# Second halves of an h block behind an eviction, a queue of weight sums that yields, norm parts in scratch columns: one change to a fused attention, mixture and SwiGLU kernel

## The chip, the cores and the metric

One core of one Trainium2 chip runs the whole program in one launch. The metric is device time in microseconds (us), the median over runs; lower is better. Five engines run their own instruction streams and wait for each other on semaphores: TensorE (PE, its weight loads PEld), VectorE (DVE), ScalarE (ACT), GpSimd (POOL) and SyncE (SP, which here only issues DMAs).

## The reference

Causal attention with a local or a strided mask on 4x8 heads of 576 tokens, then a dense mixture of 8 experts whose gate is balanced by Sinkhorn steps (layer 1), then RMS norm and SwiGLU (layer 2). The 2304 tokens of 512 features run through

```
h = np.maximum(x @ w1[e], 0.0)              # layer 1: 8 experts, 512 -> 1024 -> 512
out += P[:, e:e+1] * (h @ w2[e])
rms = np.sqrt(np.mean(x * x, axis=-1) + 1e-6)
xn = x / rms * rms_g                        # norm
g, val = xn @ w_gate, xn @ w_val            # layer 2: 512 -> 1536 -> 512
return (g / (1 + np.exp(-g)) * val) @ w_out
```

Products are taken to float32's precision: each operand is a high and a low part, and three matmuls (high x high, high x low, low x high) make one product.

## The kernel before, in words

Attention and expert 0 come first; experts 1 to 7 and layer 2 then run in one loop over *quads*. A quad (g, qd) is expert or pass g on a third qd of the tokens (768, six tiles of 128, laid out as 2x2 blocks of 384 columns and 256 features). Layer 1 has 7 x 3 quads; layer 2 has 3 passes (g = 8, 9, 10) x 3 quads. A Strassen-like scheme computes four h blocks of 128 x 384 with seven products instead of eight: that is a *chain*, and the table `PROD` says for each of its seven products, here called product 0 to 6, which sum of weight blocks (`w1t`, `w1x`: "w1 sums") and which sum of x blocks (`xt`, `xx`: seven slots, loaded from the scratch tensor `xnd` in device memory in layer 2) it takes, and into which of two PSUM banks (`ub`) it adds. Consecutive chains swap the banks, and the next chain starts to write a bank as soon as the last reader of the old chain is through with it.

`outcome` runs behind each product. Products 0, 2 and 3 only have their bank copied away by ScalarE (`keep`). Behind products 1, 4, 5 and 6 an h block is finished: its number n is 0, 2, 1 and 3. In layer 1 that is an *add* of bank and keep on VectorE (n = 0, 2, 1; block 3 is read from the bank itself), a *high* part with relu on ScalarE, and a *low* part, the difference, on VectorE. In layer 2 a *round* is two chains. The g chain makes an add, a sigmoid on ScalarE and a product with it on VectorE; the v chain makes an add, a product with the g chain's block ("mul", L1084), a high part on ScalarE and a low part on VectorE (L1033). The engine that is asked for the second half of a block stands right behind the first in program order, whatever else it could do meanwhile.

The twelve products of a round's h blocks with w2 ("downs", L701 to L703, banks `db` 0 to 5) are laid between the products of the next round. So a quad's last downs run in the first round of the next quad, and VectorE *evicts* the six banks (L1465, L1476) into `acc` there. Everything else is pumped from queues, one slot after every product and down: `prep` makes the next chain's w1 sums from raw weights that GpSimd's DMAs bring (seven VectorE steps a block), `prep2` makes w2 parts, `conv` converts float64 weights, and `norm` does the norm steps between the layers: for each tile m of a quad, sums `ta`, `tb` and their high and low parts (VectorE, ScalarE, GpSimd), stored to `xnd` by SP. Behind expert 7 these parts lie in two free x slots before the store; the x loads of the next quad go into the same slots, so they wait until the stores have read them.

The lines of the profile that the next parts use: product L1019; add L1062 (layer 1), L1071 (g) and L1082 (v); mul L1074 (g) and L1084 (v); low part L1037 (layer 1) and L1033 (v); keep copies L1047; w1 sums L860 and L863; x loads L950; norm parts L1129, norm stores L1137 and L1156.

Of the kernel before, what the change touches and what calls it, by code (L numbers as in the profile page):

```python
# [22 lines left out]


class Background:


    def __init__(self):
        self.tasks = []
        self.queues = []  # L30
        self.now = 0

# [34 lines left out]
class Queue:  # L67


    def __init__(self, clock):  # L70
        self.clock = clock
        self.items = []
        self.last = 0
        clock.queues.append(self)
# [4 lines left out]
    def run(self):  # L79
        self.last = min(max(self.last + self.items[0][1], self.clock.now - 1), self.clock.now)  # L80
        self.items.pop(0)[2]()

    def pump(self):
        while self.items and self.last + self.items[0][1] < self.clock.now:
            self.run()

    def drain(self, tag):
        while any(x[0] == tag for x in self.items):
            self.run()


@with_exitstack
def kernel(
# [22 lines left out]
    NG = 4  # L116
# [71 lines left out]
    prep, prep2, conv = Queue(bg), Queue(bg), Queue(bg)  # L188
# [516 lines left out]
    def up(ps, w, x, n):  # L705
        for c in range(KC):
# [6 lines left out]
            )  # L713
            if c % 2:
                bg.pump()

    def down(accs, h, w, first, last, t):
# [6 lines left out]
        )  # L724

# [62 lines left out]
    def convert(nm, f, half):  # L788
# [15 lines left out]
        def head():  # L804
# [3 lines left out]
            )  # L808

        def number():  # L810
# [6 lines left out]
            )  # L817

        def tail():
# [3 lines left out]
            )  # L823

        def whole():
            nc.vector.tensor_tensor(out=t, in0=a.bitcast(F32), in1=t, op=ALU.add)

# [18 lines left out]
    def combine(s, raw):  # L846
# [18 lines left out]
        def first():  # L865
            round_(raw[:, :512], 0, 2)
            sum_(s1, a21, a22, ALU.add)

        def second():
            round_(a22, 2, 1)  # L870
            rest(a11, 0, 1)
            rest(a12, 1, 1)

        def third():
            sum_(a21, a11, a21, ALU.subtract)
            sum_(s2, s1, a11, ALU.subtract)

        def fourth():
            round_(tmp, 3, 2)
            rest(a22, 2, 1)  # L880
            sum_(a12, a12, s2, ALU.subtract)

        def fifth():
            round_(a21, 5, 1)
            rest(tmp, 3, 2)

        def sixth():
            round_(a12, 6, 1)
            rest(a21, 5, 1)

        def seventh():
            rest(a12, 6, 1)

# [29 lines left out]
    def prepare_2(g, f):  # L923
# [12 lines left out]
        def low():  # L936
            nc.vector.tensor_tensor(out=w2t[:, i, 1], in0=t, in1=w2t[:, i, 0].bitcast(F32), op=ALU.subtract)

# [77 lines left out]
    def product(ps, w, x, first):  # L1016
        for c in range(2):
            for n, (i, k) in enumerate(((0, 0), (0, 1), (1, 0))):
# [3 lines left out]
                )  # L1022

# [4 lines left out]
    def scratch(i):  # L1028
        return fa[:, 3200 + TH * i : 3200 + TH * (i + 1)] if i < 5 else cv[:, TH * (i - 5) : TH * (i - 4)]

    def put(src, h):
        nc.scalar.activation(h[0], src, AF.Copy)
        nc.vector.tensor_tensor(out=h[1], in0=src, in1=h[0].bitcast(F32), op=ALU.subtract)  # L1033

    def put_relu(src, h):
        nc.scalar.activation(h[0], src, AF.Relu)  # L1036
        nc.vector.scalar_tensor_tensor(  # L1037
            out=h[1], in0=src, scalar=0.0, in1=h[0].bitcast(F32), op0=ALU.max, op1=ALU.subtract
        )

    def outcome(i, a, b, use):


        keep = [fa[:, 2048 + TH * n : 2048 + TH * (n + 1)] for n in range(3)]
        a, b = a[:, :TH], b[:, :TH]
        if i in (0, 2, 3):
            nc.scalar.copy(keep[(0, None, 1, 2)[i]], b if i == 3 else a)  # L1047
        elif i == 1:
            use(0, b, keep[0])
        elif i == 4:  # L1050
            use(2, a, keep[2])
        elif i == 5:
            use(1, b, keep[1])
# [3 lines left out]
    def hidden_1(hs):  # L1057
# [9 lines left out]
    def hidden_g():  # L1067
# [10 lines left out]
    def hidden_v(hs):  # L1078
        def use(n, ps, more):
            src, to = ps, scratch(5 + n % 2)  # L1080
            if more is not None:
                nc.vector.tensor_tensor(out=to, in0=ps, in1=more, op=ALU.add)  # L1082
# [7 lines left out]
    def norm_scale(t0):  # L1090
# [6 lines left out]
        def mean():  # L1097
            nc.vector.tensor_scalar(out=ss, in0=ss, scalar1=1.0 / DM, scalar2=1e-6, op0=ALU.mult, op1=ALU.add)

# [3 lines left out]
        def xn(t):  # L1103
            nc.vector.tensor_scalar(
                out=acc[:, t0 + t], in0=acc[:, t0 + t], scalar1=ss[:, t : t + 1], scalar2=None, op0=ALU.mult
            )

# [3 lines left out]
    def norm_turn(ps, t):  # L1111
# [5 lines left out]
        )  # L1117

    def norm_blocks(qd, i, spare, close):
# [3 lines left out]
        ta, tb = cv[:, 768:1024], cv[:, 1024:1280]  # L1123
        sa, sb, sc = *spare, xt_flat[:, 7680:8192]
# [6 lines left out]
        def plain():  # L1131
            parts(xa, sa[:, :512], sa[:, 768:1280])
            parts(b22, sa[:, 512:768], sa[:, 1280:1536])

# [521 lines left out]
```

## Time and profile before

| what | us |
|---|---|
| median of 3 runs (2116.95 to 2119.74) | 2118.75 |
| span of the profiled execution | 2113.9 |
| TensorE busy | 2076.4 (98%) |
| VectorE busy | 1215.6 (58%) |
| ScalarE busy | 747.2 (35%) |
| GpSimd busy | 333.0 (16%) |

The profiled execution has no time of its own beside its span; the median of the runs is 4.85 us above it, and that difference stands for what lies around the span. "Busy" is an engine's time in instructions. TensorE's matmuls are pipelined: one of 128 x 384 is drawn 0.33 us long, but the next starts 0.174 us after it, so a busy TensorE is not one at its peak, and an idle gap that the trace draws is shorter than the delay behind it.

### The profile page before, as it was taken

To read this page: it belongs to the slowest core of one execution; us is meant where nothing else is said; L and a number is where in the kernel's file an instruction comes from. 1 tells how busy PE (TensorE), PEld (TensorE's weight loads), DVE (VectorE), ACT (ScalarE), POOL (GpSimd) and SP (SyncE) were. 2 spreads that over 40 slices of the span, in tenths; PEclk is the share of its full clock that TensorE was granted. 3 is DMA by queue.
4 is the path that set the end of the run, shared out by engine and by line. 5 is a ranking of instruction groups with operands and counts; after the bars stand their busy time and mean duration, and the time that the engine had idled before them with its cause. 6 is when DMAs were issued, how large, how long until landed. Compare 5 with 4: busy or idle time off the path is not lost.

```text
span 2113.9 us, 30671 instructions
## 1 busy us (share of the span) xinstructions
PE 2076.4 (98%) x11343; PEld 1853.1 (88%) x11343; DVE 1215.6 (58%) x2669; ACT 747.2 (35%) x1763; POOL 333.0 (16%) x503
## 2 busy tenths in 40 slices
PE   8999999999999999999999999999999999999999
PEld 7888888888888888888888988888988799888888
DVE  4777647557446644754664466455357665546645
ACT  7856323223223322322332233223244444423322
POOL 6444211123101200210120021001012100100000
PEclk9999999999999999999999999999999999999999
DMA  7685565553355253434623552552265674254242
GB/s 195 171 217 144 163 217 168 192 175 107 120 169 167 73 184 130 148 120 136 199 85 131 166 167 77 172 192 60 85 180 160 228 239 145 71 188 146 99 165 90
DMA packets 293861, 319.24 MB, mean 151 GB/s; under 512 B 80016, under 2 KB 215376, under 8 KB 293712
## 3 DMA queue, kind: packets, MB, share of 16 engines
q1 hardware_dynamic: 271568, 247.86, 37.5%
q0 software_dynamic: 22144, 69.42, 10.5%
q8 instruction: 89, 1.46, 0.3%
q14 instruction: 60, 0.49, 0.1%
HBM read 237.78 MB, written 79.43 MB: 150 GB/s over the span
## 4 chain that ended last, share of the span: by engine, by line
PE 83%; DVE 9%; ACT 3%; DMA 2%; issue 2%; SPq 0%; POOL 0%; DVEq 0%; ACTq 0%; POOLq 0%
PE ub L1019 36%; PE db L702 12%; PE db L703 12%; PE db L701 12%; PE psh L701 2%; PE psh L702 1%; PE psh L703 1%; DVE cv L1084 1%; PE psy L701 1%; PE ps_s L471 1%; PE psy L702 1%; PE psy L703 1%; DVE acc L1465 1%; DVE cv L1082 1%; PE ps_o L540 1%
## 5 line engine op out<-in xcount | busy, mean ns | idle before, releaser
L1019 PE MATMUL ub<-xt,w1t 128*128 128x384 f32 x2000 | 494.9, 339 | 15.5 <-DVE cv L1084 4.7
L1019 PEld LDWEIGHTS ub<-xt,w1t 128*128 128x128 f32 x2000 | 366.0, 188 | 66.6 <-DVE cv L1084 8.7
L1019 PE MATMUL ub<-xx,w1t 128*128 128x384 f32 x1600 | 393.9, 338 | 4.5 <-DVE hx L1037 1.4
L1019 PEld LDWEIGHTS ub<-xx,w1t 128*128 128x128 f32 x1600 | 292.0, 188 | 42.9 <-DVE cv L1084 3.8
L1062 DVE TENSOR_TENSOR fa<-ub,fa 128x384 f32<-128x384 f32 x252 | 139.9, 555 | 277.0 <-PE ub L1019 275.9
L1047 ACT COPY fa<-ub 128x384 f32<-128x384 f32 x360 | 171.3, 476 | 334.7 <-PE ub L1019 332.8
L1019 PE MATMUL ub<-xt,w1x 128*128 128x384 f32 x808 | 272.2, 337 | 0.0
L703 PE MATMUL db<-w2t,ht 128*128 128x512 f32 x644 | 255.4, 397 | 0.0
L702 PE MATMUL db<-w2t,ht 128*128 128x512 f32 x644 | 254.6, 395 | 0.0
L701 PE MATMUL db<-w2t,ht 128*128 128x512 f32 x644 | 250.7, 389 | 0.0
L703 PE MATMUL db<-w2t,hx 128*128 128x512 f32 x612 | 243.8, 398 | 0.0
L702 PE MATMUL db<-w2t,hx 128*128 128x512 f32 x612 | 242.0, 395 | 0.0
L701 PE MATMUL db<-w2t,hx 128*128 128x512 f32 x612 | 240.8, 394 | 0.8 <-DVE acc L1114 0.7
L1019 PE MATMUL ub<-xx,w1x 128*128 128x384 f32 x632 | 212.6, 336 | 0.0
L1036 ACT ACTIVATE hx<-fa 128x384 fp32r<-128x384 f32 x126 | 66.2, 525 | 261.9 <-DVE fa L1062 260.7
L1036 ACT ACTIVATE ht<-fa 128x384 fp32r<-128x384 f32 x126 | 66.2, 525 | 261.8 <-DVE fa L1062 261.8
L1019 PEld LDWEIGHTS ub<-xt,w1x 128*128 128x128 f32 x808 | 152.0, 188 | 0.0
L703 PEld LDWEIGHTS db<-w2t,ht 128*128 128x128 f32 x644 | 120.6, 187 | 26.0
L703 PEld LDWEIGHTS db<-w2t,hx 128*128 128x128 f32 x612 | 114.6, 187 | 26.8 <-DVE hx L1033 2.4
L701 PEld LDWEIGHTS db<-w2t,ht 128*128 128x128 f32 x644 | 121.0, 188 | 11.0
L702 PEld LDWEIGHTS db<-w2t,ht 128*128 128x128 f32 x644 | 120.8, 188 | 11.0
L701 PEld LDWEIGHTS db<-w2t,hx 128*128 128x128 f32 x612 | 115.1, 188 | 13.0 <-DVE acc L1114 2.1
(218 smaller groups left out, 3080.7 us busy)
## 6 DMA issues: line engine op xcount, KB each, us to landing
fa<-in_moe_w_dram POOLq DMA_DIRECT2D x112, 256.0 KB, 3.5
xt<-xdt SPq DMA_DIRECT2D x32, 768.0 KB
xx<-xdt SPq DMA_DIRECT2D x28, 768.0 KB
xt<-xnd SPq DMA_DIRECT2D x28, 768.0 KB
y1d<-acc SPq DMA_DIRECT2D x72, 256.0 KB
acc<-y1d SPq DMA_DIRECT2D x72, 256.0 KB
xx<-xnd SPq DMA_DIRECT2D x21, 768.0 KB
xt<-xdh SPq DMA_DIRECT2D x50, 192.0 KB
```

Source lines behind the costliest of these rows:

```text
L471: nc.tensor.matmul(ps[:mq, i * nk : (i + 1) * nk], z[:, n, :, :].rearrange("p h c -> p (h c)"), t[:, c0 : c0 + nk], start=True, stop=True,)
L540: nc.tensor.matmul(ps[D * h : D * h + D, n * w : (n + 1) * w], st["v"][:nk, h, n, :], st["pt"][:nk, c0 : c0 + w], start=True, stop=True,)
L701: nc.tensor.matmul(ps, lh, rh, start=first, stop=False)
L702: nc.tensor.matmul(ps, lh, rl, start=False, stop=False)
L703: nc.tensor.matmul(ps, ll, rh, start=False, stop=last)
L1019: nc.tensor.matmul(ps[:, :TH], w[i][:, c], x[:, k, c], start=first and c == 0 and n == 0, stop=c == 1 and n == 2, skip_group_check=True,)
L1036: nc.scalar.activation(h[0], src, AF.Relu)
L1047: nc.scalar.copy(keep[(0, None, 1, 2)[i]], b if i == 3 else a)
L1062: nc.vector.tensor_tensor(out=src, in0=ps, in1=more, op=ALU.add)
L1082: nc.vector.tensor_tensor(out=to, in0=ps, in1=more, op=ALU.add)
L1084: nc.vector.tensor_tensor(out=to, in0=src, in1=scratch(n), op=ALU.mult)
L1465: nc.vector.scalar_tensor_tensor(out=a, in0=db[b], scalar=prob[:, ti, g : g + 1], in1=a, op0=ALU.mult, op1=ALU.add)
```

## The change

Three things. First, a queue `fin`, pumped ahead of the others, takes the second half of a block (low part, product with the sigmoid, high part of the v chain), with a lag of 0 or 1 slot; it is forced out before a down that reads the block, before the next chain's second product (block 3 of the chain before), and before the block's next turn. The sums of an h block stay in the keep columns, the sigmoid goes into the keep columns too, and only block 3 of a v chain uses `cv`. Second, a queue may yield: `prep` runs no step while a running count of VectorE's work (columns + 150 for each instruction) is more than 1500 ahead of a count of TensorE's, from expert 7 on, unless over 8 items wait; `prep.drain` at the chain's start still forces what that chain needs. Third, the norm parts behind the first two quads of expert 7 go to `fa` columns 3200 to 4992, `cv` columns 0 to 1280 (the sums `ta` and `tb` are stored from where they lie) and the end of `xt`, in five second stores for each tile where there were three, and the next quad's first two x loads are issued as its last round begins.

```diff
 class Background:
+    def matmuls(self, n, columns):
+        self.pe += n * (columns * 2 // 5 + 13)
+
+    def vector(self, columns):
+        if columns:
+            self.dve = max(self.dve, self.pe) + columns + 150
+
+    def room(self):
+        return not self.tight or self.dve <= self.pe + AHEAD
...
 class Queue:
     def pump(self):
-        while self.items and self.last + self.items[0][1] < self.clock.now:
+        while self.items and self.last + self.items[0][1] < self.clock.now and (not self.yields or len(self.items) > 8 or self.clock.room()):
             self.run()
...
+    def follow(self, steps, tag=None):
+        if not self.items:
+            self.last = max(self.last, self.clock.now)
+        self.add(steps, tag)
...
-    prep, prep2, conv = Queue(bg), Queue(bg), Queue(bg)
+    fin, prep, prep2, conv = Queue(bg), Queue(bg, True), Queue(bg), Queue(bg)
...
     def hidden_1(hs, side):
         def use(n, ps, more):
             src = ps
             if more is not None:
-                src = scratch(n)
-                nc.vector.tensor_tensor(out=src, in0=ps, in1=more, op=ALU.add)
-            put_relu(src, hs[n])
+                src = more
+                with_more(src, ps, more)
+            high(src, hs[n], AF.Relu)
+            fin.follow([(0 if more is None else 1, lambda: low_relu(src, hs[n]))], (n, side))
...
+    def hidden_g(side):
         def use(n, ps, more):
-            src, to, s = ps, scratch(n), scratch(4)
+            src, to = ps, scratch(n)
+            s = scratch(4) if more is None else more
...
             nc.scalar.activation(s, src, AF.Sigmoid)
-            nc.vector.tensor_tensor(out=to, in0=src, in1=s, op=ALU.mult)
+            def times():
+                nc.vector.tensor_tensor(out=to, in0=src, in1=s, op=ALU.mult)
+                return TH
+            fin.follow([(0 if more is None else 1, times)], (n, side))
...
+    def hidden_v(hs, side):
         def use(n, ps, more):
-            src, to = ps, scratch(5 + n % 2)
+            h = hs[n]
+            to = cv[:, :TH] if more is None else more
+            def times(src=to):
+                nc.vector.tensor_tensor(out=to, in0=src, in1=scratch(n), op=ALU.mult)
+                return TH
             if more is not None:
-                nc.vector.tensor_tensor(out=to, in0=ps, in1=more, op=ALU.add)
-                src = to
-            nc.vector.tensor_tensor(out=to, in0=src, in1=scratch(n), op=ALU.mult)
-            put(to, hs[n])
+                with_more(to, ps, more)
+                fin.follow([(0, times)], (n, side))
+            else:
+                bg.vector(times(ps))
+            fin.follow([(0 if n in (1, 3) else 1, lambda: high(to, h)), (1, lambda: low(to, h))], (n, side))
...
     def keep2():
-            for k, n, s, t in ((3, 4, 0, sb[:, :1024]), (3, 2, 1, sb[:, 1024:]), (5, 2, 1, sc)):
+            for s, k, n, t in stores:
...
     def down_one(d):
+            fin.drain((i, hs[i] // 4))
...
     def evict(n, b):
+            if g in (E - 1, E):
+                norm.drain("blocks")
...
                 def ahead(i, last):
-                    if not last or i != late_i:
+                    if not last or i != -1:
                         return
                     if j == rounds - 1:
-                        if g >= E - 1:
-                            norm.drain("blocks")
                         if fresh:
                             for k in (0, 1):
                                 load_block(nmap[k], g2 >= E, qd2, k)
...
                     for i, (wk, xk, which, begins) in enumerate(PROD):
+                        if i == 1:
+                            fin.drain((3, 0))
+                            fin.drain((3, 1))
                         product((a, b)[which], w_block(s, wk), x_view(xmap[xk]), begins)
...
                     if g0 == E - 1 and j0 == NF // 2 - 1:
+                        ends = [xt_flat[:, 7680 + 256 * i : 7936 + 256 * i] for i in range(2)]
...
-                            spare = [x_slot(i) for i in free]
+                            sa, last = fa[:, 3200:4736].bitcast(F32R), fa[:, 4736:4992].bitcast(F32R)
+                            parts = [cv[:, 256 * i : 256 * (i + 1)].bitcast(F32R) for i in range(5)]
+                            highs, lows = parts[:3] + [last], [ends[0], parts[3], parts[4], ends[1]]
+                            stores = [
+                                (0, 0, 3, cv[:, :768].bitcast(F32R)), (0, 3, 1, last), (1, 0, 1, ends[0]),
+                                (1, 1, 2, cv[:, 768:1280].bitcast(F32R)), (1, 3, 1, ends[1]),
+                            ]
```

How this moves instructions on an engine is decided by the queues, so three places of the built programs are shown. First VectorE at the end of a v chain of pass 10 that evicts nothing. Before (`ub_4208` and `ub_4207` are the two banks; L1082 add, L1084 mul, L1033 low part; blocks 2, 1 and 3 in turn):

```order
L1082 TENSOR_TENSOR cv<-ub_4208,fa 128x384
L1084 TENSOR_TENSOR cv<-cv,fa 128x384
L1033 TENSOR_TENSOR ht<-cv,ht 128x384
L1082 TENSOR_TENSOR cv<-ub_4207,fa 128x384
L1084 TENSOR_TENSOR cv<-cv,fa 128x384
L1033 TENSOR_TENSOR ht<-cv,ht 128x384
L1084 TENSOR_TENSOR cv<-ub_4208,fa 128x384
L1033 TENSOR_TENSOR ht<-cv,ht 128x384
```

The same place of the changed kernel (L1082 add, L1136 mul, L1072 low part):

```order
L1082 TENSOR_TENSOR fa<-ub_4208,fa 128x384
L1136 TENSOR_TENSOR fa<-fa 128x384
L1082 TENSOR_TENSOR fa<-ub_4207,fa 128x384
L1072 TENSOR_TENSOR ht<-fa,ht 128x384
L1136 TENSOR_TENSOR fa<-fa 128x384
L1072 TENSOR_TENSOR ht<-fa,ht 128x384
L1136 TENSOR_TENSOR cv<-ub_4208,fa 128x384
L1072 TENSOR_TENSOR ht<-cv,ht 128x384
```

The low part of block 2 now stands behind the add of block 1; the blocks 2 and 1 no longer pass through `cv`.

Second VectorE at the end of the first round of the last quad, in which the quad before it is evicted. Before (L1476 evictions of `db` 0, 1 and 2 into `acc`):

```order
L1476 TENSOR_TENSOR acc<-db_3960,acc 128x512
L1082 TENSOR_TENSOR cv<-ub_4208,fa 128x384
L1084 TENSOR_TENSOR cv<-cv,fa 128x384
L1033 TENSOR_TENSOR hx<-cv,hx 128x384
L1476 TENSOR_TENSOR acc<-db_3961,acc 128x512
L1082 TENSOR_TENSOR cv<-ub_4207,fa 128x384
L1084 TENSOR_TENSOR cv<-cv,fa 128x384
L1033 TENSOR_TENSOR hx<-cv,hx 128x384
L1476 TENSOR_TENSOR acc<-db_3962,acc 128x512
L1084 TENSOR_TENSOR cv<-ub_4208,fa 128x384
```

The same place of the changed kernel (L1546 evictions):

```order
L1546 TENSOR_TENSOR acc<-db_3960,acc 128x512
L1082 TENSOR_TENSOR fa<-ub_4208,fa 128x384
L1136 TENSOR_TENSOR fa<-fa 128x384
L1546 TENSOR_TENSOR acc<-db_3961,acc 128x512
L1082 TENSOR_TENSOR fa<-ub_4207,fa 128x384
L1072 TENSOR_TENSOR hx<-fa,hx 128x384
L1136 TENSOR_TENSOR fa<-fa 128x384
L1546 TENSOR_TENSOR acc<-db_3962,acc 128x512
L1072 TENSOR_TENSOR hx<-fa,hx 128x384
L1136 TENSOR_TENSOR cv<-ub_4208,fa 128x384
```

The low part of block 2 has moved behind the eviction and the next add, that of block 1 behind the last eviction.

Third SP's DMAs around the last norm tile before layer 2 begins. Before (`xnd<-xt` norm stores, `acc<-y1d` sums of the experts so far, `xt<-xnd` and `xx<-xnd` x loads of the first quad of layer 2, then of the next):

```order
L1137 DMA xnd<-xt 128x6x128 x2
L1156 DMA xnd<-xt 128x8x128
L1156 DMA xnd<-xt 128x4x128 x2
L1492 DMA acc<-y1d 128x512 x2
L950 DMA xt<-xnd 128x2x768 x3
L950 DMA xx<-xnd 128x2x768 x4
```

The same place of the changed kernel (L1200 and L1221 stores, L984 x loads):

```order
L1200 DMA xnd<-fa 128x6x128 x2
L984 DMA xt<-xnd 128x2x768 x2
L1221 DMA xnd<-cv 128x6x128
L1221 DMA xnd<-fa 128x2x128
L1221 DMA xnd<-xt 128x2x128
L1221 DMA xnd<-cv 128x4x128
L1221 DMA xnd<-xt 128x2x128
L1563 DMA acc<-y1d 128x512
L984 DMA xt<-xnd 128x2x768
L1563 DMA acc<-y1d 128x512
L984 DMA xx<-xnd 128x2x768 x4
```

Two of the seven x loads now stand ahead of the last tile's second stores, and those stores read `cv` and `fa` instead of `xt`.

## Rows read from the trace of the kernel before

**Rows 1.** The page: span, and busy time of each engine

```profile
span 2113.9 us, 30671 instructions
...
PE 2076.4 (98%) x11343; PEld 1853.1 (88%) x11343; DVE 1215.6 (58%) x2669; ACT 747.2 (35%) x1763; POOL 333.0 (16%) x503
```

**Rows 2.** TensorE's waits, 1500:2114: line, releaser, us in total, times, longest

```profile
PE ub L1019 <- DVE cv L1084: 6.0, 8, 1.8
PE ub L1019 <- DVE cv L1082: 3.9, 3, 1.7
...
PE ub L1019 <- DVE fa L1074: 1.2, 3, 0.5
PE ub L1019 <- DVE hx L1037: 0.7, 1, 0.7
PE db L701 <- DVE acc L1114: 0.7, 1, 0.7
PE ub L1019 <- DVE fa L1062: 0.5, 1, 0.5
```

**Rows 3.** TensorE's waits, 380:1590, same columns

```profile
PE ub L1019 <- DVE hx L1037: 2.6, 7, 0.4
```

**Rows 4.** Timeline of TensorE around a v chain's end: start, duration, instruction, idle before

```profile
2051.52 0.33 PE L1019 MATMUL ub<-xx,w1x 128*128 128x384 f32 x1
...
2054.96 0.40 PE L703 MATMUL db<-w2t,ht 128*128 128x512 f32 x1
2055.43 0.61 PE L1019 MATMUL ub<-xt,w1t 128*128 128x384 f32 x2
...
2057.06 0.40 PE L703 MATMUL db<-w2t,ht 128*128 128x512 f32 x1
2057.30 0.51 PE L1019 MATMUL ub<-xt,w1t 128*128 128x384 f32 x2
```

**Rows 5.** Timeline of VectorE at the same place

```profile
2051.93 0.56 DVE L1033 TENSOR_TENSOR ht<-cv,ht 128x384 fp32r<-128x384 f32 x1 [0.59 <-ACT ht L1032]
2052.41 0.55 DVE L1082 TENSOR_TENSOR cv<-ub,fa 128x384 f32<-128x384 f32 x1
...
2054.15 0.56 DVE L1033 TENSOR_TENSOR ht<-cv,ht 128x384 fp32r<-128x384 f32 x1 [0.59 <-ACT ht L1032]
2054.81 0.56 DVE L1084 TENSOR_TENSOR cv<-ub,fa 128x384 f32<-128x384 f32 x1
```

**Rows 6.** TensorE: first product of layer 2, of its last chain, first down behind that

```profile
1653.87 0.33 PE L1019 MATMUL ub<-xt,w1t 128*128 128x384 f32 x1
...
2089.98 0.51 PE L1019 MATMUL ub<-xx,w1t 128*128 128x384 f32 x2
...
2101.58 0.39 PE L701 MATMUL db<-w2t,ht 128*128 128x512 f32 x1
```

**Rows 7.** TensorE: two product starts of layer 2's first chain

```profile
1659.43 0.59 PE L1019 MATMUL ub<-xt,w1t 128*128 128x384 f32 x2 [1.88 <-DMA xt<-xnd]
...
1661.39 0.58 PE L1019 MATMUL ub<-xx,w1t 128*128 128x384 f32 x2
```

**Rows 8.** Windows: length, engines' busy time, granted clock, DMA share, GB/s

```profile
1630.00:1632.00 2.00, 2.00 (x12) 1.83 (x11) 1.97 (x4) 1.41 (x4) 2.00 (x3) 1.00 0.20 58
1660.00:1666.00 6.00, 6.00 (x30) 4.75 (x29) 3.37 (x9) 3.15 (x7) 0.00 (x0) 1.00 1.03 400
1686.00:1689.40 3.40, 3.27 (x11) 3.18 (x12) 2.08 (x6) 1.70 (x5) 0.86 (x1) 0.50 0.00 0
```

**Rows 9.** TensorE behind w1 sums and behind an eviction; VectorE at g block 3

```profile
1834.05 0.61 PE L1019 MATMUL ub<-xx,w1t 128*128 128x384 f32 x2 [0.57 <-DVE cv L1084]
...
1931.91 0.62 PE L1019 MATMUL ub<-xt,w1t 128*128 128x384 f32 x2 [0.56 <-DVE cv L1084]
...
1669.69 0.56 DVE L1074 TENSOR_TENSOR fa<-ub,fa 128x384 f32<-128x384 f32 x1 [0.62 <-ACT fa L1073]
```

**Rows 10.** VectorE: first w1 sum behind a raw load

```profile
1657.54 0.42 DVE L863 TENSOR_TENSOR fa<-fa 128x256 f32<-128x256 f32 x1 [3.09 <-DMA fa<-m2v]
```

More of the change, by code (lines that the diff above doesn't have):

```diff
@@ L67, with __init__ @@
 class Queue:
-    def __init__(self, clock):
+    def __init__(self, clock, yields=False):
         self.clock = clock
+        self.yields = yields
         self.items = []
@@ L713, in up @@
             )
+            bg.matmuls(3, n)
             if c % 2:
@@ L724, in down @@
         )
+        bg.matmuls(3, DM)
     hturn, oturn = [0], [0]
@@ L1022, in product @@
                 )
+        bg.matmuls(6, TH)
     def h_slot(i):
@@ L1028, in scratch, with high, low, low_relu @@
     def scratch(i):
-        return fa[:, 3200 + TH * i : 3200 + TH * (i + 1)] if i < 5 else cv[:, TH * (i - 5) : TH * (i - 4)]
-    def put(src, h):
-        nc.scalar.activation(h[0], src, AF.Copy)
+        return fa[:, 3200 + TH * i : 3200 + TH * (i + 1)]
+    keeps = [fa[:, 2048 + TH * n : 2048 + TH * (n + 1)] for n in range(3)]
+    def high(src, h, func=AF.Copy):
+        nc.scalar.activation(h[0], src, func)
+    def low(src, h):
         nc.vector.tensor_tensor(out=h[1], in0=src, in1=h[0].bitcast(F32), op=ALU.subtract)
-    def put_relu(src, h):
-        nc.scalar.activation(h[0], src, AF.Relu)
+        return TH
+    def low_relu(src, h):
         nc.vector.scalar_tensor_tensor(
@@ L1039, in put_relu, with with_more, hidden_1 @@
         )
+        return TH
+    def with_more(out, ps, more):
+        nc.vector.tensor_tensor(out=out, in0=ps, in1=more, op=ALU.add)
+        bg.vector(TH)
     def outcome(i, a, b, use):
-        keep = [fa[:, 2048 + TH * n : 2048 + TH * (n + 1)] for n in range(3)]
         a, b = a[:, :TH], b[:, :TH]
+        for side in range(2):
+            fin.drain(((0, 0, 1, 2, 2, 1, 3)[i], side))
         if i in (0, 2, 3):
-            nc.scalar.copy(keep[(0, None, 1, 2)[i]], b if i == 3 else a)
+            nc.scalar.copy(keeps[(0, None, 1, 2)[i]], b if i == 3 else a)
         elif i == 1:
-            use(0, b, keep[0])
+            use(0, b, keeps[0])
         elif i == 4:
-            use(2, a, keep[2])
+            use(2, a, keeps[2])
         elif i == 5:
-            use(1, b, keep[1])
+            use(1, b, keeps[1])
         else:
             use(3, a, None)
-    def hidden_1(hs):
+    def hidden_1(hs, side):
         def use(n, ps, more):
@@ L1452, in down_one @@
             )
+            bg.matmuls(3, DM)
             if ends:
@@ L1533 @@
                 fresh = n + 1 < len(quads) and not again and j == rounds - 1
-                late_i = 0 if g == E - 1 else -1
                 if n == 0 and j == 1:
@@ L1576 @@
                         ahead(i, ci == len(chains) - 1)
-                        if fresh and ci == len(chains) - 1 and i >= late_i:
+                        if fresh and ci == len(chains) - 1:
                             for x in range(min(i, 4) + 1):
@@ L1612 @@
                     if g0 == E - 1 and j0 == NF // 2 - 1:
+                        ends = [xt_flat[:, 7680 + 256 * i : 7936 + 256 * i] for i in range(2)]
                         if g == E:
-                            spare = w2t[:, NG:].rearrange("p f s n -> p (f s n)")
-                            spare = [spare[:, 1536 * i : 1536 * (i + 1)] for i in range(2)]
-                        else:
-                            spare = [x_slot(i) for i in free]
+                            sa, sb = (
+                                w2t[:, NG:].rearrange("p f s n -> p (f s n)")[:, 1536 * i : 1536 * (i + 1)] for i in range(2)
+                            )
+                            parts = [sb[:, 256 * i : 256 * (i + 1)] for i in range(6)]
+                            highs, lows = parts[:4], parts[4:] + ends
+                            stores = [(0, 0, 4, sb[:, :1024]), (1, 0, 2, sb[:, 1024:]), (1, 2, 2, xt_flat[:, 7680:8192])]
+                        else:
+                            sa, last = fa[:, 3200:4736].bitcast(F32R), fa[:, 4736:4992].bitcast(F32R)
[5 more added lines that the diff above has]
+                            ]
+                        spare = sa, highs, lows, stores
                         turning = (qd0, spare)
```

47 lines of the change are left out of this document (36 added, 11 removed).

## The prediction

> **What bounds the kernel now.** I read the page first: TensorE is busy for 2076.4 of 2113.9 us, VectorE for 1215.6 [rows 1]. At 98% only TensorE's waits and restarts can be won, so the next view is the list of its waits. Up to expert 6 it shows one regular kind: seven waits, 2.6 us together, all for the low part L1037 of block 3, once at each of seven quad ends [rows 3]. From 1500 on the waits are longer, and nearly all name VectorE: 8 for the mul L1084, 3 for the add L1082, 3 for the product with the sigmoid L1074 [rows 2]; one of 1.88 is for an x load [rows 7].
>
> What does such a wait cost? The reader compares two places with the same instructions. From a down's last matmul to the next product it is 2057.30 − 2057.06 = 0.24 without a wait, and 2055.43 − 2054.96 = 0.47 with one that is drawn as 0.07 (the down ends at 2055.36); the first pair of matmuls then takes 0.61 where it takes 0.51 [rows 4]. So a wait costs what is drawn and some 0.16 + 0.1, 0.27 in all.
>
> In layer 2 the loss can be measured as a whole. The last chain, in which nothing waits, runs from 2089.98 to 2101.58, 11.60 us. From the first product at 1653.87 to the same end are 36 chains, 447.7 us [rows 6], against 36 x 11.60 = 417.6, and the six transposed tiles at about 0.45 add 2.7: 27.4 us are lost there. In layer 1 the seven quad ends lose 2.6 + 7 x 0.27 = 4.5. The three waits of expert 7's last quad (L1037 0.7, L1114 0.7, L1062 0.5 [rows 2]) lose 1.9 + 3 x 0.27 = 2.7, with a short fourth 3.1. **35.0 us is all that this change could bring**: nothing it does makes a matmul shorter.
>
> **The change, part by part.** It adds no instruction to VectorE, ScalarE or TensorE; SP gets twelve DMAs more. All else is order and buffers.
>
> *Halves behind other work.* At a v chain's end without evictions, the add of block 1 could start when its product is through, 2051.52 + 0.33 = 2051.85 [rows 4], but VectorE stands at the low part of block 2, idle for 0.59, until 2051.93, and adds at 2052.41. Block 3's mul, for which TensorE's next product waits, comes at 2054.81 behind another idle 0.59 [rows 5]. In the new order I replay this with the same durations: add 2051.97, low part of 2 at 2052.45, mul 2052.93, and the low part of 1, which waits for ScalarE as before, 2054.08. The mul of block 3 then follows 0.48 later, the pitch of 2051.93 to 2052.41, not 0.66 as from 2054.15 to 2054.81, since it no longer writes the `cv` columns that the low part reads: 2054.56. It ends at 2055.12, and with the 0.06 that lie between 2055.37 and 2055.43 now, the product could start at 2055.18; undisturbed it would start at 2054.96 + 0.24 = 2055.20. That is no margin to speak of. Eight such boundaries cost 0.07 + 0.27 = 0.34 each, 2.7; I count half as left, 1.4.
>
> Where a round evicts, the new order puts an eviction or the next add into each idle 0.59. At 1931.91 TensorE waits 0.56 for the mul of block 3 behind an eviction [rows 9]; filling two gaps of 0.59 brings that mul some 1.1 us forward. The waits for adds and muls of v chains are 3.9 + 6.0 = 9.9 in 11 [rows 2]; without the one of 1.8 below they are 8.1 in 10, with 10 x 0.27 10.8 lost. All but those near 1831 (below) stand at evictions and should go. From g to v chains the product of block 3 with its sigmoid, at 1669.69, comes after 0.62 idle [rows 9], since all four sigmoids share one scratch and the third must wait for the second's reader; separate columns remove that. Three such boundaries show 1.2 [rows 2] and lose 2.0, six more are like the plain ones at 0.34: 4.1, which should go. In layer 1 the low part of block 3 stood behind one such gap, and 0.4 is the most that it came late: 4.5 gone.
>
> *w1 sums that yield.* At 1834.05 TensorE waits 0.57 for a mul behind w1 sums [rows 9], after a wait for an add behind others; by replay some of these sums still lie between, and I leave 0.8. What yields must come later. The built order has one place where the sums of a block are forced out at once, five instructions at about 0.4 (one takes 0.42 [rows 10]), 2 us in a chain of 11.60 whose VectorE work ends 0.6 to 1 us before it is needed: no charge.
>
> *Norm parts and x loads.* At layer 2's start TensorE waits 1.88 for an x load and then starts a product each 1.96 us (1659.43, 1661.39) [rows 7]; the DMA engines' share is 1.03 and they move 400 GB/s [rows 8], by which a load of 768 KB takes 1.97. A product with its down takes 1.76 undisturbed, so five products behind loads lose 1.88 + 0.27 + 4 x 0.20 = 2.95. With two loads ahead of the last tile's second stores, 2 x 1.97 = 3.9 us of transfer move to a stretch where the share was 0.20 at 1630 to 1632 [rows 8]. That is more than what is lost; I leave 0.5, since it was higher again soon after. The price: the sums of tile m+1 write `ta` and `tb`, from which tile m's stores now read. Four times VectorE has to wait for a DMA, and behind it on VectorE stand layer 1's adds and low parts, for which TensorE waits. No row shows a store's landing. The bounds are nothing and, each, the 3.09 that VectorE once waited for a raw load [rows 10], 12.4 for four. The sum comes two pumped slots after the store, 1.8 us (a slot is 0.7 behind a down, 1.07 behind a product), which leaves 1.3 a time; I take it that one of four falls where TensorE has no reserve: 1.3.
>
> By the Trainium skill ("DMA: Bandwidth & Descriptors", Anatomy of one DMA) a transfer has a fixed cost of about 2 us, most of it the receipt of the write before the semaphore moves. An estimate by that page is a wait of 0.2 for each of the four at least, and more with five stores queued where three were, as each is issued after the other. The trace bears out only that landings are slow under load, in the 3.09 above. By the page alone the term would be between 0 and 0.8 instead of 1.3.
>
> *The clock.* At 1684.60 TensorE waits 1.8 (the longest L1084 [rows 2]), behind three norm scalings and an eviction on VectorE; soon after, at 1686.00 to 1689.40, the granted clock is 0.50, that is 1.2 GHz of 2.4 [rows 8], worth half of 3.4, 1.7. With 1.8 + 0.27 the stretch loses 3.8. Replay leaves a wait of 1.4 in it; of the clock I leave 0.3 x 1.7 = 0.5, because a wait as long at 1659.43 was followed by full clock in 1660 to 1666 [rows 8].
>
> **The sum.** Of 35.0 there stay: x loads 0.5, stretch at 1684 1.4 + 0.5, 1831 0.8, plain boundaries 1.4, expert 7's last quad 0.5, store landings 1.3, and 0.6 of what I can assign to no place (27.4 − 2.95 − 10.8 − 2.7 − 4.1 − 3.8 = 3.0, most of it near the evictions, where a wait behind a down costs more than 0.27): 7.0. The gain is 28.0, the span 2113.9 − 28.0 = 2085.9. The median lies 4.85 above the span now, so 2090.8.
>
> **Rivals.**
> *Half.* VectorE waits for every store (5.2 instead of 1.3), the loads stay paced by the DMA engines (2.95 instead of 0.5), the plain boundaries keep their 2.7, the stretch at 1684 its 3.8: 3.9 + 2.45 + 1.3 + 1.9 = 9.6 less, 2100. For it: a replay with a margin of 0.02, a DMA share already at 1.03, and TensorE's faster pace, which leaves VectorE less time everywhere. Against: the gaps at evictions and sigmoids, some 13, do not depend on any of these.
>
> *Nothing.* TensorE waits for block 3's mul because of the seven products' own spacing, and VectorE's new order just moves its idle time; then only the loads and one or two long waits gain, 0 to 5: 2114 to 2119. Against: the 0.59 is named as ScalarE's in each row, and work for the gap stood behind it.
>
> *Slower.* Yielding sums come out in one piece where a chain begins, and TensorE waits for weights. The next raw load is issued only after the sums before it have read their buffer, so a late block costs 3.09 of landing [rows 10] and eleven VectorE instructions at 0.42, 4.6: 7.7 us. It decides from the fourth block (28 / 7.7 = 3.6); with all eight of passes 9 and 10 it is 62 − 28 = 34 slower, 2153. For it: the yield lets up to 8 items pile up. Against: only one forced place in the built order, and VectorE idle over 40% of the time.
>
> **How the numbers follow.** Forecast 0.64, 2084 (all 35.0) to 2097; half 0.23, 2097 to 2113; nothing 0.08; slower 0.05. A change within 0.2%, 4.2 us, is about what a measurement cannot tell from none: of "nothing" 0.05 lies there and 0.03 on the faster side. Faster: 0.64 + 0.23 + 0.03 = 0.90. The range 2084 to 2108 holds the forecast and most of half, about 0.8.
>
> **What would show it.** In the list of waits after 1500, L1082 and the product with the sigmoid should be gone and the mul have at most some 4 us; the seven waits up to 1590 should be gone. Layer 2 from first product to last down should take about 425 (417.6 + 2.7 + 5.2) instead of 447.7. A second TensorE product at layer 2's start that still waits over 1 us for `xnd` refutes the loads' step; VectorE rows at the norm sums with idle time before them that ends on a DMA from `cv`, over 1.5 us each, mean the half case; waits of a product for w1 parts mean the slower one.

## The result and the profile after

The changed kernel takes 2085.53 us (median of 4 runs, 2085.12 to 2087.52), the kernel before 2117.99 beside it (4 runs): ratio 0.9851, 95% interval 0.9837 to 0.9865, some 32 us faster. The prediction was 2090.8 in a range of 2084 to 2108.

The page of the changed kernel, span and busy time of each engine:

```profile
span 2083.4 us, 30578 instructions
...
PE 2062.2 (99%) x11343; PEld 1854.3 (89%) x11343; DVE 1209.7 (58%) x2669; ACT 751.6 (36%) x1763; POOL 333.2 (16%) x503
```

Against [rows 1] VectorE is about as busy as it was; the span is 30.5 shorter. TensorE's waits in the changed kernel, 1500 to the end, which answer to [rows 2] (line, releaser, us in total, times, longest):

```profile
PE ub L1053 <- ACT fa L1092: 1.0, 2, 0.8
PE db L723 <- DVE hx L1072: 0.7, 1, 0.7
PE ub L1053 <- DVE hx L1076: 0.2, 1, 0.2
```

Adds, muls, sigmoids and x loads are gone from the list; of 380 to 1590 [rows 3] nothing is left. New are a keep copy (L1092) and a low part (L1072). The ends of the stretch of layer 2 that [rows 6] shows, on TensorE (start, duration, instruction):

```profile
1647.20 0.51 PE L1053 MATMUL ub<-xt,w1t 128*128 128x384 f32 x2
...
2071.31 0.39 PE L721 MATMUL db<-w2t,ht 128*128 128x512 f32 x1
```

That is 424.1 for 36 chains, where it was 447.7.

The time up to one down near the start of the quads differs between the profiled executions of all kernels here: it begins between 380.01 and 385.35. Of the change only the order of a few VectorE instructions from 324 us on lies ahead of it, and at 316 us, ahead of those, the executions already differ by 4.2. Parts of a few us are therefore measured below inside the profiled executions, from this down to the last matmul. In the trace of before and in that of the changed kernel these two are

```profile
380.01 0.39 PE L701 MATMUL db<-w2t,hx 128*128 128x512 f32 x1
...
2109.55 0.39 PE L703 MATMUL db<-w2t,ht 128*128 128x512 f32 x1
```

```profile
380.12 0.39 PE L721 MATMUL db<-w2t,hx 128*128 128x512 f32 x1
...
2079.29 0.39 PE L723 MATMUL db<-w2t,ht 128*128 128x512 f32 x1
```

so this "stretch" is 1729.54 before and 1699.17 after: **30.37 gained**. It is one execution each, and the waits for DMAs in it move: `shared` (below) is the changed kernel, instruction for instruction, up to layer 2, and is 0.8 behind it there. So a part under 1 us is shown only where the place of the loss is shown too.

### The profile page after: what moved, and what is told of

Its sections match the earlier page's. It is cut to its first block, busy times and chain, and to the rows that moved or that the text cites. A ratio compares the mean times of both kernels' runs of the same rounds, so it can differ in the third digit from the quotient of the medians.

```text
span 2083.4 us, 30578 instructions
## 1 busy us (share of the span) xinstructions
PE 2062.2 (99%) x11343; PEld 1854.3 (89%) x11343; DVE 1209.7 (58%) x2669; ACT 751.6 (36%) x1763; POOL 333.2 (16%) x503
## 3 DMA queue, kind: packets, MB, share of 16 engines
q0 software_dynamic: 22144, 69.42, 10.8%
## 4 chain that ended last, share of the span: by engine, by line
PE 92%; DVE 3%; DMA 2%; ACT 2%; issue 1%; POOL 1%; SPq 0%; POOLq 0%; ACTq 0%; DVEq 0%
PE ub L1053 40%; PE db L723 13%; PE db L722 13%; PE db L721 13%; PE psh L721 2%; PE psh L723 2%; PE psh L722 2%; PE psy L721 1%; PE ps_s L491 1%; PE psy L722 1%; PE psy L723 1%; PE ps_o L560 1%; PE ps_t L435 1%; PE ps_p L547 1%; DVE fa L1082 0%
## 5 line engine op out<-in xcount | busy, mean ns | idle before, releaser
L1082 DVE TENSOR_TENSOR fa<-ub,fa 128x384 f32<-128x384 f32 x360 | 200.3, 556 | 403.6 <-PE ub L1053 399.6
L1092 ACT COPY fa<-ub 128x384 f32<-128x384 f32 x360 | 172.1, 478 | 364.0 <-PE ub L1053 363.3
L1069 ACT ACTIVATE ht<-fa 128x384 fp32r<-128x384 f32 x153 | 80.4, 526 | 305.9 <-DVE fa L1082 248.7
L1069 ACT ACTIVATE hx<-fa 128x384 fp32r<-128x384 f32 x153 | 80.5, 526 | 291.2 <-DVE fa L1082 248.2
```

The costliest lines, as they stand in the source:

```text
L1069: nc.scalar.activation(h[0], src, func)
L1082: nc.vector.tensor_tensor(out=out, in0=ps, in1=more, op=ALU.add)
L1092: nc.scalar.copy(keeps[(0, None, 1, 2)[i]], b if i == 3 else a)
```

## Experiments

The theory: the three parts of the change add up, and most comes from halves that no longer hold VectorE while ScalarE works. The rivals: VectorE's backlog of w1 sums was the cause; or the new columns were; or the parts need each other.

**Leaving out one part.** `no_yield`:

```diff
-    fin, prep, prep2, conv = Queue(bg), Queue(bg, True), Queue(bg), Queue(bg)
+    fin, prep, prep2, conv = Queue(bg), Queue(bg), Queue(bg), Queue(bg)
```

> The changed kernel, but the queue of w1 sums does not yield. Theory (the order of the second halves does most of it): the sums stand ahead of adds and muls again only near 1831, 1929 and 1980 of before; TensorE loses 1 to 3 us there, time 2086.5 to 2088.5. Rival (VectorE's backlog of w1 sums was the cause of the long waits, which lost 1.9 + 3.1 + 3.7 there): most of these 8.7 us come back, about 2093.

Measured: 2089.04 (2087.75 to 2090.15), stretch 1702.68, 3.5 lost, a little more than the theory had, far less than the rival. Some 3.1 of it are lost at boundaries where w1 sums meet chain ends, as expected. Besides, layer 2's first chain is 1.6 slower (1.3 of it comes back later, where the changed kernel waits for a store: a price of the yield, below). There is a wait in it that I had not thought of, for an x load. In this kernel's timeline of TensorE:

```profile
1654.74 0.41 PE L1053 MATMUL ub<-xx,w1t 128*128 128x384 f32 x1 [0.82 <-DMA xx<-xnd]
```

A w1 sum that yields also keeps its raw buffer, so the next raw loads are issued later: two that GpSimd issues 3.2 and 2.6 ahead of layer 2's first product here go out 6.4 and 6.9 behind it in the changed kernel. What the DMA engines move in the 5 us behind that product, here and then in the changed kernel (queue: packets, MB, share; q1 are SP's transfers, q0 the raw loads):

```profile
q1 hardware_dynamic: 477, 1.21, 62.9%
q0 software_dynamic: 236, 0.77, 39.6%
```

```profile
q1 hardware_dynamic: 618, 1.76, 90.0%
q0 software_dynamic: 80, 0.26, 13.1%
```

By the Trainium skill ("DMA: Bandwidth & Descriptors", Issuing engines are not separate DMA queues) transfers that different engines issue share the same 16 DMA engines and interleave; the trace agrees, with 1.98 MB here and 2.02 there, whichever queue they belong to. But the raw loads are not the only difference: SP issues the third x load 3.9 ahead of that product here and 6.0 ahead of it in the changed kernel. In `ahead_600` (below), where the two raw loads go out later still, it is issued 5.2 ahead, and a product waits 0.5 for an x load. How much of the wait is the raw loads' and how much the later issue's is not shown.

`no_norm`: norm parts go to the x slots and loads start late, as before.

```diff
-                    if not last or i != -1:
+                    if not last or i != late_i:
...
-                            sa, last = fa[:, 3200:4736].bitcast(F32R), fa[:, 4736:4992].bitcast(F32R)
...
+                            sa, sb = (x_slot(i) for i in free)
```

> The changed kernel with norm parts in the free x slots and the first x loads behind them, as before. Theory: TensorE waits for the third load again and starts a product every 1.96 us, 2.8 lost, and about 1 more in the last quad of expert 7; time 2088.5 to 2090. Rival (the loads were late only because everything else was): under 0.5 us, 2085.5 to 2086.

Measured: 2088.03 (2085.91 to 2089.1), stretch 1701.26, 2.1 lost. Up to the end of layer 2's first five products it is 1.5 behind the changed kernel; in expert 7's last quad it is 0.5 ahead, where no sum of VectorE waits for a store of `cv` (it waits 0.8 for one of `xt`, which TensorE does not notice). `spread` (below), which has the stores of `cv`, is 0.45 ahead there too, so this is not the places' price alone. The pace is back (products start 1.95, 1.97 and 2.12 apart), the long wait for the third load is not. So loads and norm places were worth about 2 in the first chain, not 2.95, and 0.7 of that is drawn as a wait for a low part, not for a load.

`no_fin`: each second half is emitted directly, with the new columns.

```diff
     def follow(self, steps, tag=None):
-        if not self.items:
-            self.last = max(self.last, self.clock.now)
-        self.add(steps, tag)
+        for _, f in steps:
+            self.clock.vector(f())
```

> The changed kernel, but each second half is emitted directly behind its first half, with the new buffers. Theory: the seven quad ends (4.4) and the waits for adds and muls at evictions (about 8) come back, the plain boundaries lose their first gap again but keep the shorter pitch of block 3's mul; time 2098 to 2103. Rival (separate columns did it, since the next add no longer waits for an old reader): 2086 to 2090.

Measured: 2105.89 (2104.62 to 2109.21), stretch 1717.22, **18.1 lost**, a little more than expected. Its list of waits after 1500 and of 390 to 1590:

```profile
PE ub L1052 <- DVE cv L1135: 4.8, 7, 1.8
PE ub L1052 <- DVE fa L1081: 1.4, 3, 0.7
PE ub L1052 <- ACT fa L1091: 1.1, 2, 0.9
PE ub L1052 <- DVE fa L1122: 0.7, 2, 0.4
```

```profile
PE ub L1052 <- DVE hx L1075: 2.6, 7, 0.4
```

The seven quad ends are back, 2.6 in 7 as in [rows 3], and 7 waits for muls (L1135). Both rivals fall, that yielding does it and that the columns do: the sums yield here too, and the columns are the new ones.

**One part alone.** `buffers` is the kernel before with the new columns only (no queue, no yield, old norm places):

> The kernel before with nothing but the new columns for an h block (sums in the keep columns, each sigmoid in its own, block 3 alone in cv), with each second half directly behind the first. Theory: the boundaries from g to v chains (4.1) and some 0.18 at each plain boundary are won, the rest stays; time 2112 to 2114 where before has 2118. Rival (columns did most of it): under 2105. Rival (columns do nothing, the sigmoids were never the bound): 2117 to 2118.

Measured: 2114.38 (2110.29 to 2118.16, 10 runs) beside 2117.93; ratio 0.9981, interval 0.9971 to 0.9991. Stretch 1724.37, 5.2 gained, where 4.1 + 8 x 0.18 = 5.5 was the sum of both effects. That the two numbers are so near is luck. 1.2 of the 5.2 lie in layer 2's first chain, where the waits for x loads are shorter than in [rows 7]:

```profile
PE ub L1052 <- DMA xx<-xnd: 0.7, 2, 0.4
```

Nothing shows that the columns did that. The other 4.0 lie at the places meant: eight plain boundaries at 0.18, and 2.6 from g to v chains, where some 1.3 stays lost (one wait of 0.4 for the product with the sigmoid, L1122, and two short ones). The larger rival falls, and so does "nothing".

`fin_only` has queue and columns, without yield and with the old norm places (the first two edits above together):

> The kernel before with the queue of second halves and the new columns, without yielding sums and with norm parts and x loads as before. Theory (the three parts add up): the two left out cost 3.5 and 2.1 against the changed kernel, so 2091 to 2092. Rival (they need each other: without room VectorE is late whatever the order of the halves): 2096 or more.

Measured: 2092.31 (2088.51 to 2094.9), stretch 1703.25, 26.3 gained. Yield and norm places bring 4.1 beside it, where leaving each out costs 3.5 + 2.1 = 5.6: they overlap, by 1.1 of it up to the end of layer 2's first chain, where 2.1 is lost against 1.7 + 1.5: both act on the same x loads. No sign that the parts need each other.

`shared` was to undo the columns under the queue:

```diff
-            s = scratch(4) if more is None else more
+            s = scratch(4)
...
-            to = cv[:, :TH] if more is None else more
+            to = cv[:, TH * (n % 2) : TH * (n % 2 + 1)]
```

> The changed kernel, but blocks 1 and 3 of a v chain (and 0 and 2) share their cv columns again and all four sigmoids share one scratch. Theory (the new columns shorten the pitch before block 3's mul from 0.66 to 0.48, and take block 3's sigmoid out of the way of an old reader): most of the 17 boundaries without evictions lose 0.25 to 0.5, 5 to 7 us in all, 2090 to 2093. Rival (with the queue the order alone is enough): 2085 to 2086.5.

Measured: 2092.38 (2091.73 to 2094.84), stretch 1704.03, 4.9 lost, a little under the theory's 5 to 7. Boundaries without evictions lose 0.17 each, where the theory had 0.25 to 0.5: that is the longer pitch ahead of block 3's mul, and the 0.18 that `buffers` wins. For the rest it settles little: with the queue a block's columns are overwritten here before its second half has used them, so part of the outputs comes from another block, and the wait for an old reader is not the one meant. 0.8 of the loss is ahead of layer 2, where the edit changes nothing.

**The bound of the yield.** `AHEAD` at 600 and at 2500:

```diff
-AHEAD = 1500
+AHEAD = 600
```

> The changed kernel with the bound from which the w1 sums yield at 600 instead of 1500. Theory: what yields earlier waits for room that is there, within 1 us of the changed kernel, 2084.5 to 2086.5. Rival (sums pile up and are forced out at chain starts, so that products wait for w1 parts, as in the slower case of the prediction): 2089 or more.

> The changed kernel with the bound from which the w1 sums yield at 2500 instead of 1500. At 600 products waited for w1 parts (4.5 lost from the first product of the quads on), without a bound adds and muls waited behind sums (3.5 lost). Theory (two costs that fall and rise with the bound): between the two, 0.5 to 2.5 lost against 1500, adds and muls of v chains named in the list of waits, w1 parts not. Rival (the model's count is no measure of lateness, 1500 is one lucky order): a loss as large as either, 3.5 or more, or a gain.

At 600: 2089.91 (2089.32 to 2090.37), stretch 1703.68, **4.5 lost**. The theory (within 1 us) falls: it is the slower rival of the prediction on a small scale. From its list of TensorE's waits after 1500:

```profile
...
PE ub L1053 <- ACT w1t L882: 1.1, 1, 1.1
PE ub L1053 <- DVE hx L1076: 0.9, 1, 0.9
...
PE ub L1053 <- DVE w1t L886: 0.7, 1, 0.7
PE ub L1053 <- DMA xx<-xnd: 0.5, 1, 0.5
```

Products wait for the parts of w1 (L882, L886) that had been put off: some 2.7 of the 4.5. Another 0.9 is the wait for an x load with the slower pace behind it. And 0.8 is a wait for a store in expert 7 (below), which is not the bound's work: `shared` loses the same there with 1500. At 2500: 2086.82 (2085.8 to 2088.75), stretch 1700.63, 1.5 lost, as much as the theory had. Its list names two waits for low parts, where the theory had adds and muls, and none for w1 parts. So the loss falls and rises with the bound: 4.5, 0, 1.5, and 3.5 without one.

**The two waits that are new.** `spread_scale` lets the three norm scalings lie a slot apart; `spread` and `spread_2` also give a tile's first norm parts a longer lag in layer 2, 3 slots and 2:

```diff
-    return steps + [(2 if t == 0 else 0, lambda t=t: xn(t)) for t in range(3)]
+    return steps + [(2 if t == 0 else 1, lambda t=t: xn(t)) for t in range(3)]
...
-        return [(0.85 if close else 1.2, f) for f in steps]
+        return [(0.85 if close else 1.2 if f is not plain else 3, f) for f in steps]
```

> The changed kernel with the three norm scalings one slot apart instead of in one piece, and a lag of 3 slots instead of 1.2 ahead of a tile's first norm parts in layer 2. Theory: the down that waits for a low part behind three scalings and an eviction (1.7 lost with what follows) and the product that waits for a keep copy behind a norm part that waits for a store (1.05) start on time; about 2 us won, 2083 to 2084. Rival (each wait goes to the next instruction in the same piece of work): 2085 to 2086.

> The changed kernel with the three norm scalings one slot apart and nothing else. From the first product of the quads to the last matmul the kernel with both edits gained 0.81 over the changed kernel: 1.3 up to the stretch of the scalings, and 0.6 lost again later, at an add that came late where the tile's first norm parts had the longer lag. Theory: without the longer lag the 0.6 comes back, 1.3 gained over that stretch, time 2084 to 2085. Rival (the late add is the scalings' own): 0.8 or less.

> The changed kernel with the norm scalings one slot apart and a lag of 2 slots ahead of a tile's first norm parts in layer 2. With 1.2 the first parts stood on ScalarE 2.11 for a store and a product lost 1.48 behind them; with 3 that wait was gone, but the last tile's parts were forced out in one piece and an add came 1.6 late. Theory (the lag only has to cover the store): two slots more than halve the wait and nothing piles up, 1 us over the kernel with the scalings spread alone, 1.5 over the changed kernel, 2083.5 to 2084.5. Rival (the late tile is always forced out together): as the version with 3, 0.8 over the changed kernel.

Medians: `spread` 2087.01, `spread_scale` 2085.0 (2082.93 to 2085.46), `spread_2` 2086.43 (2085.2 to 2087.16). Between these and 2085.53 the runs tell nothing, since the part ahead of the quads differs more (the down at 380.12 stands at 382.56 in the profile of `spread_2`). The stretch does: 1698.36, 1698.71 and 1697.69, that is 0.8, 0.5 and **1.5** gained over the changed kernel. Of `spread`'s 0.8, 0.45 lies ahead of layer 2, at a store wait in expert 7; the other two, with the same scalings there, are 0.1 ahead and 0.2 behind at that point.

The scalings are worth the same in all three: around them each is 0.9 faster than the changed kernel. The rest differs. The theory of `spread`, 2 won, missed. `spread_scale` gave the rival's number for another reason. It starts the product behind the scalings 1.0 earlier, and loses half of it again at a keep copy behind a norm part that waits for a store; this store lands 0.56 later after its issue than in the changed kernel. ScalarE, then TensorE in `spread_scale`:

```profile
1704.65 0.42 ACT L1190 ACTIVATE w2t<-acc 128x256 fp32r<-128x256 f32 x1 [2.11 <-DMA xnd<-w2t]
1704.97 0.46 ACT L1092 COPY fa<-ub 128x384 f32<-128x384 f32 x1
```

```profile
1705.49 0.45 PE L1053 MATMUL ub<-xt,w1t 128*128 128x384 f32 x1 [1.32 <-ACT fa L1092]
```

With 3 slots and with 2 ScalarE waits only 0.40 for the store, and TensorE is not drawn to wait there. With 3 the last tile's parts then stand together on VectorE ahead of an add for which TensorE waits 1.4; with 2 they stand together too, but end 1.2 earlier against TensorE, and no add is late: the theory's 1.5, the shortest stretch of all kernels here. That the lag did it is not shown. ScalarE's wait is 1.71 shorter than in `spread_scale`; the lag puts the norm part 0.36 later, and the other 1.35 come from the store, which lands 7.45 after its issue in `spread_scale` and 6.10 here (on this store see below).

## Why the prediction held, and where its sum was off

*What bounds it; the ceiling.* Right: the waits were the time. Of 35.0 that could be won the stretch won 30.37; 28.0 was forecast.

*The offset.* I added 4.85 for what lies around the span. It is 2.1 in runs of the kernel before (2115.92 with a span of 2113.8) and 1.86 in the changed kernel (2085.26 with 2083.4). The profiled execution of before was simply a short one: the spans of its other runs here go from 2112.8 to 2120.5. That is 2.8 to 3 of the 5.3 by which 2090.8 was too high; the sum itself was 2.4 off. Some luck is in that: terms that were 3.8 too high together stand against one of 1.4 that it lacked (the keep copy, below).

*Plain boundaries, 1.4 left: mis-sized, 0.2.* The eight lose nothing any more; the 0.2 is at another v chain's end, at 1699.69, where norm parts stand between the halves. VectorE and TensorE of the changed kernel at the place of [rows 4, 5]:

```profile
2023.35 0.56 DVE L1082 TENSOR_TENSOR fa<-ub,fa 128x384 f32<-128x384 f32 x1 [0.54 <-PE ub L1053]
2023.83 0.55 DVE L1072 TENSOR_TENSOR ht<-fa,ht 128x384 fp32r<-128x384 f32 x1
2024.29 0.55 DVE L1136 TENSOR_TENSOR fa<-fa 128x384 f32<-128x384 f32 x1
2025.44 0.56 DVE L1072 TENSOR_TENSOR ht<-fa,ht 128x384 fp32r<-128x384 f32 x1 [0.59 <-ACT ht L1069]
2025.91 0.55 DVE L1136 TENSOR_TENSOR cv<-ub,fa 128x384 f32<-128x384 f32 x1
```

```profile
2022.98 0.33 PE L1053 MATMUL ub<-xx,w1x 128*128 128x384 f32 x1
...
2026.42 0.40 PE L723 MATMUL db<-w2t,ht 128*128 128x512 f32 x1
2026.65 0.51 PE L1053 MATMUL ub<-xt,w1t 128*128 128x384 f32 x2
```

The replay was right row by row: add, +0.48, +0.94 (0.96 forecast), +2.09 (2.11), +2.56 (2.59). Only the add starts 0.04 behind its product (2022.98 + 0.33), not 0.12. The mul ends at 2026.46, and with the same 0.06 the product could start at 2026.52, 0.13 ahead of the 2026.65 at which it does: a margin, though a thin one.

*Evictions, sigmoids, quad ends, all gone:* right. `no_fin` puts 18.1 on the order of the halves, `buffers` 4.0 on the columns at their places. At the boundaries from g to v chains the reason was half right: columns alone win 2.6 of the 4.1 there, and the rest goes only with the queue.

*Yield, 0.8 left at its place:* about right (0.6 lost there); leaving the yield out costs 3.5, of which I had priced only the 1.1 at that place, and counted the rest under evictions.

*x loads, 0.5 left: 0.* The first chain's products start undisturbed (start on TensorE, then the DMA share of three windows: length, busy, clock, share, GB/s):

```profile
1654.24 0.51 PE L1053 MATMUL ub<-xx,w1t 128*128 128x384 f32 x2
...
1656.01 0.51 PE L1053 MATMUL ub<-xx,w1t 128*128 128x384 f32 x2
```

```profile
1640.00:1650.00 10.00, 10.00 (x52) 8.99 (x51) 5.65 (x13) 4.48 (x9) 1.62 (x3) 1.00 1.05 380
1650.00:1660.00 10.00, 10.00 (x54) 9.32 (x53) 5.62 (x11) 4.18 (x9) 1.06 (x2) 1.00 1.03 398
1660.00:1666.00 6.00, 6.00 (x32) 5.46 (x31) 4.97 (x11) 3.40 (x9) 0.00 (x0) 1.00 0.18 67
```

1.77 apart instead of the 1.96 of [rows 7]. The DMA engines are as full as in [rows 8], but done by 1660 to 1666, where they were at 1.03 before. By `no_yield` and `no_norm` both the yield and the norm places are needed for that; the prediction had given it to the places and the early loads alone.

*Store landings, 1.3, and expert 7's last quad, 0.5: together about 0.75* (of the 3.1 priced there 2.36 were won). The waits of VectorE exist, one of them long, and TensorE sees the end of it (VectorE, then TensorE of the changed kernel):

```profile
1630.77 0.42 DVE L1206 TENSOR_TENSOR cv<-acc 128x256 f32<-128x256 f32 x1 [1.15 <-DMA xnd<-cv]
```

```profile
1633.86 0.61 PE L1053 MATMUL ub<-xx,w1t 128*128 128x384 f32 x2 [0.18 <-DVE hx L1076]
```

That is 0.45 lost here. `spread` loses nothing at this place and `shared` 1.3, so the term moves from execution to execution, and the 1.3 taken is its upper end.

The prediction had no row for a store's landing. The trace's semaphore events of the changed kernel now give one, from the issue in expert 7's last quad to the last of 16 DMA engines: 3.6 to 5.0 us for the stores of the first two tiles, 6.3 to 8.8 for those of the last. The 2 us that the prediction takes from the Trainium skill ("DMA: Bandwidth & Descriptors", Anatomy of one DMA) are given there for transfers that GpSimd issues. These are SP's, beside x loads, and took longer; the measurement decides.

*The stretch at 1684, 1.4 + 0.5: 1.7 + 0.* The wait moved: not the product but a down now waits, for a low part that stands behind three scalings and an eviction (VectorE, then TensorE of the changed kernel):

```profile
1670.37 1.27 DVE L1164 TENSOR_SCALAR acc<-acc,cv 128x512 f32<-128x512 f32 x3
1671.56 0.74 DVE L1534 SCALAR_TENSOR_TENSOR acc<-db,prob,acc 128x512 f32<-128x512 f32 x1
1672.22 0.55 DVE L1072 TENSOR_TENSOR hx<-fa,hx 128x384 fp32r<-128x384 f32 x1
```

```profile
1672.83 0.50 PE L723 MATMUL db<-w2t,hx 128*128 128x512 f32 x1 [0.73 <-DVE hx L1072]
```

That is the price of the queue: a half that is put behind other work stands behind all of it. The granted clock stays at 1.00 from 1672 to 1680. It fell in `buffers` at the same place as before (a mean of 0.53 from 1690.2 to 1693.6), not in `no_fin` nor in `fin_only`. `no_fin` has the wait of 1.8 at the same place, so that wait by itself is not what brings it down. Either the yield with the earlier loads or the reordered halves suffice to keep it up, and why it falls stays open.

*What the sum had nothing for:* a keep copy behind a norm part that waits for a store at 1705 (ScalarE idle 1.55, TensorE 0.78), which with a late add behind it costs 1.4. TensorE's faster pace does not explain it: in `no_yield`, which is there 11 ahead of before, ScalarE waits for no store, and in `no_fin`, only 6.6 ahead, it waits 1.68. What differs is when the store lands whose source the part writes again. ScalarE and TensorE of the changed kernel, and the raw loads that GpSimd issues 11 ahead of the store:

```profile
1705.15 0.42 ACT L1190 ACTIVATE w2t<-acc 128x256 fp32r<-128x256 f32 x1 [1.55 <-DMA xnd<-w2t]
```

```profile
1705.99 0.62 PE L1053 MATMUL ub<-xt,w1t 128*128 128x384 f32 x2 [0.78 <-ACT fa L1092]
```

```profile
1687.07 1.13 POOL L942 DMA_DIRECT2D fa<-m2g  x2 [10.52 <-DVE w1x L886]
```

SP issues the store, 512 KB, at 1698.24, and by the trace's semaphore events the last of 16 DMA engines lands its share 6.89 later. In the nine kernels whose w1 sums yield this takes 6.01 to 7.53, in the four others 3.95 to 5.68. In the nine, two raw loads of 256 KB are issued 10.8 to 12.4 ahead of the store (in the changed kernel once a w1 sum has read their buffer), and move 0.5 MB among SP's transfers; in the four no raw load is issued in the 18 us ahead of it. So this term is a price of the yield, which the sum did not have. That the raw loads are what holds up the store is argued: no run moves them alone.

The rivals: "half" asked for load-paced products, waits for every store and plain boundaries that stay; only the second came, in part. "Nothing" fell. "Slower" has its mechanism, shown at 600, and does not start at 1500: no wait for w1 parts is in the list.

## What to carry to other kernels

Where an engine asks another for a result and takes it up at once, put the next independent instruction between the two: the queue for this was worth 18 of 30 us here, though VectorE was busy for only 58% of the time. Then look for what the queue now puts *ahead* of a result that someone waits for. And measure a sum against the stretch that the change touches, not against a median that contains another stage's variation.

## What the runs showed of the hardware

A yield on VectorE reached the DMA engines: sums that wait keep their raw buffer, its next load comes later, and at 2.0 MB in 5 us SP's loads moved 1.76 MB instead of 1.21; a wait of 0.82 for an x load went with it, though SP's issues also came 2.1 earlier. A store of 512 KB landed 3.95 to 5.68 us after its issue in the four kernels without the yield and 6.01 to 7.53 in the nine with it, at the same place; the first of its 16 DMA engines was done after 3.46 to 4.36 in all of them, and ScalarE waited up to 2.19 for the last. The time around the span was 1.7 to 2.2 us in 86 of 91 runs and 2.8 to 3.0 in the others, and the first 316 us, with the same instructions on TensorE, VectorE, ScalarE and GpSimd, varied by 4.2 between the thirteen profiled executions.
